# Pooled attention followed by a residual MLP: the first batch issued in single steps from a written list, with the token weights loaded in two transfers

## The chip, the cores and the metric

The kernel runs on one core of a Trainium2 chip. The metric is the device time of one execution in microseconds (us), taken as the median of several runs. A core has five engines that run their own instruction streams and wait for each other through semaphores: TensorE (PE, with its weight loads shown as PEld), VectorE (DVE), ScalarE (ACT), GpSimd (POOL) and SyncE (SP). Transfers between HBM and on-chip memory are issued by SP, ACT and POOL and carried out by 16 transfer engines. A transfer that also changes the type (float32 in HBM, bfloat16 on chip) is issued by GpSimd here.

## The reference, cut to what matters

```python
def attn(q, k, v):                       # each (8 batches, 8 heads, 576, 64), float32
    k_p = k.reshape(B, H, 72, 8, D).mean(axis=3)      # 8 keys pooled into one
    v_p = v.reshape(B, H, 72, 8, D).mean(axis=3)
    scores = (q @ k_p.T) / 8             # 576 x 72 a head
    attn = exp(scores - max) / sum       # softmax
    return attn @ v_p

x = attn(q, k, v) as (8, 576, 512)       # heads side by side
a1 = alpha1 * x + beta1
tok = einsum('ts,bsd->btd', w_tok, a1)   # tokens mixed, w_tok is 576 x 576
u = x + lam * tok
a2 = alpha2 * u + beta2
out = u + lam * (max(a2 @ w_ch1, 0) @ w_ch2)          # 512 -> 2048 -> 512
```

## The kernel before, in words

Tokens are laid out in chunks of 128 rows; a batch has four chunks and a rest of 64 rows, and two batches share one chunk for their rests. Four chunks make a block, and the MLP runs over nine blocks. The main loop (from line 1198) issues block n's MLP and, in between, the attention and token mixing of batch n + 1: each piece of work has a due time written beside it, the pieces are sorted by it, and each is issued whole. Everything before that loop, lines 1054 to 1135, is the first batch: its attention and mixing have no MLP beside them, and their order is the order of the calls. This part is what the change rewrites. Engines run their instructions in the order in which they are issued, so the place of a call sets the place on each engine that it uses.

The pieces of the first batch:

- `att_F` (line 580) transposes a quarter of q on TensorE and copies the result out of PSUM; `att_Frem` does it for the rest rows. `double_k` (629) copies a column of k on VectorE, which the pooling of k needs, and for the first half also converts the rest of k.
- `att_K` (663) pools four heads of k on TensorE (16 small matmuls and 4 for the rest) into one PSUM tile, which two copies move to `kpT`. `first_V` (690) does the same for v.
- `att_S` (712) makes one head's scores: two halves, each a matmul of 256 columns (the second with 64 more for the rest) and one exponential on ScalarE. 16 exponentials make the first batch.
- `att_AV` (773) multiplies with v and normalises on VectorE (`reciprocal`, then `tensor_tensor`) into `x`. `att_X` (801) and `rest_X` (794) multiply x with lam*alpha1, which `spread_lamal` (499) has broadcast to all rows by a float32 matmul and a copy. The results `xs` are the operands of token mixing.
- `setup_wtok` (514) transposes 128 rows of the token weights on TensorE (five transposes) and copies them to `wtT`; `setup_rowsum` (527) adds a row of sums. `setup_vectors` (506) turns beta2 and alpha2 into columns.
- `mix_T` (862) mixes tokens for a chunk: five matmuls of 512 columns, an add on VectorE into `u`, then a scaling with alpha2 into bfloat16 on VectorE or GpSimd. `mix_uT` (881) transposes that chunk for the MLP.
- `mlp_A` (906) makes 128 of the hidden columns; in block 0 it is called for the first 256 tokens (the first half, with a bias column) and the other 256 (the second half, with the activation).

Transfers: all that convert types go through GpSimd's queue, in the order of its calls: the first batch's q, k and v (lines 409 to 447), the token weights (`load_wtok`, 386), the first half of w_ch1 (`load_w1(0)`), the second batch's q and k, the second and third part of w_ch1, the second batch's v (`load_v32`), w_ch2. They use eight completion semaphores in turn, so a transfer also waits until the eighth before it has landed. The second batch's k goes into buffers of the first batch's k and has to wait until that has been pooled; GpSimd's own arithmetic stands behind such an issue in the same queue. Small vectors, the broadcasts of alpha2 and lam and the rests come through SP and ACT (`load_al2`, `load_lam`, `load_rem`; a one-column memset on an engine sets from when they may start).

PSUM has eight banks: six of the pool `psA`, which `gp` (line 240) hands out in turn, and two of `psB`.

Of the kernel before, what the change touches and what calls it, by code (L numbers as in the profile page):

```python
# [7 lines left out]
FP = mybir.dt.float32  # L8
# [6 lines left out]
P = 128  # L15
SPG = 72
# [194 lines left out]
def kernel(  # L211
# [27 lines left out]

    def gp(name):  # L240
        return psA.tile([P, 512], FP, tag="gp", name=name)

# [143 lines left out]
    def load_wtok():  # L386
        nc.gpsimd.dma_start(out=wt_bf[:, 0:4 * S],
                            in_=moe_w_tok[0:512, :].rearrange("(p c) s -> p (c s)", c=4))
        nc.vector.memset(wt_bf[:, 5 * S:], 0.0)
        nc.vector.memset(wt_bf[64:128, 4 * S:5 * S], 0.0)  # L390
        nc.gpsimd.dma_start(out=wt_bf[0:REM, 4 * S:5 * S], in_=moe_w_tok[512:576, :])
# [107 lines left out]
    def spread_lamal(half, copy):  # L499
# [3 lines left out]
        nc.tensor.matmul(out=ps, lhsT=ones_row, rhs=vecs[0:1, 2, cols])  # L503
        copy(out=lamal_bc[:, cols], in_=ps)

    def setup_vectors():
        ps = gp("ps_vec")
        nc.tensor.transpose(out=ps[:, 0:8], in_=b2row, identity=identity[0:8, 0:8])
        nc.scalar.copy(out=b2c_bf, in_=ps[:, 0:4])
        nc.scalar.copy(out=al2_cols, in_=ps[:, 4:8])  # L510
        u_fm[0] = work.tile([P, 4, 2, 258], BF, tag="u_fm", bufs=3, name="u_fm")
        nc.scalar.copy(out=u_fm[0][:, :, 0, 256], in_=ps[:, 0:4])

    def setup_wtok(tcx, copy):
# [5 lines left out]
        for sc in range(5):  # L520
            nc.tensor.transpose(out=ps_w[0:P, trc * sc:trc * sc + trc],
                                in_=strided[:, sc, :] if sc < 4 else w[:, 512:640],
                                identity=identity_bf[0:trc, 0:trc])
        copy(out=wtT[:, 0:5, P * tcx:P * tcx + trc],  # L524
             in_=ps_w[:, 0:5 * trc].rearrange("p (s t) -> p s t", t=trc))

    def setup_rowsum(tcx):
# [4 lines left out]
        for sc in range(5):  # L532
            nc.tensor.matmul(out=ps[:, 0:trc], lhsT=ones_bf if sc < 4 else ones_lo,
                             rhs=wtT[:, sc, cols], start=(sc == 0), stop=(sc == 4))
        nc.scalar.copy(out=wtT[64:65, 4, cols], in_=ps[64:65, 0:trc])
# [44 lines left out]
    def att_F(b, hp, copy=nc.scalar.copy):  # L580
# [4 lines left out]
        if r == 0:  # L585
# [14 lines left out]
        def finish(copy):  # L600
            copy(out=st["qT"][u][:, 4 * r:4 * r + 4, :],
                 in_=ps_q[:, 0:512].rearrange("p (c t) -> p c t", c=4))

        if copy is None:
            return finish
        finish(copy)

    def att_Frem(b, copy=None):
# [14 lines left out]
        for c in range(2):  # L623
            nc.tensor.transpose(out=ps_q[:, 128 * c:128 * c + 128],
                                in_=st["rem"][0][:, c].rearrange("p h d -> p (h d)"),
                                identity=identity_bf)
        copy(out=st["rem_qT"], in_=ps_q[:, 0:256].rearrange("p (c t) -> p c t", c=2))

    def double_k(u):

        nc.vector.tensor_copy(out=st1[0]["k"][u][:, :, 4], in_=st1[0]["k"][u][:, :, 0])
        if u == 0:
            cast_rem_k(nc.vector)
# [29 lines left out]
    def att_K(b, u, copy):  # L663
# [18 lines left out]
        if b:  # L682
            copy(out=kp_pool[u], in_=kp)
            return
        for a in range(2):
            rows = slice(64 * a, 64 * a + 64)
            (copy or (nc.scalar.copy, nc.vector.tensor_copy)[a])(
                out=kpT_pool[u][rows, a], in_=kp[rows])

    def first_V(b, u, copy=nc.vector.tensor_copy):  # L690
# [8 lines left out]
        for c in range(nr):  # L699
            nc.tensor.matmul(out=vp, lhsT=pool_vr if b else pool_vr[0:32],  # L700
                             rhs=rest[:, heads, c], start=False,
                             stop=(c == nr - 1))
        copy(out=vp1_pool[u][:, :, 0:64], in_=vp.rearrange("p (h d) -> p h d", h=4))
# [8 lines left out]
    def att_S(b, h):  # L712
        st = st1[b]
        u, r, hh = h // 4, h // 2 % 2, h % 2
        ET = ET_pool[u][:, h % 4]
        for half in range(2):
            n0, n = 256 * half, 256 + 64 * half
            ps_sc = gp("ps_sc")
            nc.tensor.matmul(out=ps_sc[0:SPG, 0:256], lhsT=kpT_pool[u][:, half, h % 4, :],
                             rhs=st["qT"][u][:, 2 * (h % 4):2 * (h % 4) + 2, :])  # L720
            if half:
                nc.tensor.matmul(out=ps_sc[0:SPG, 256:320], lhsT=kpT_pool[u][:, hh, h % 4, :],
                                 rhs=st["rem_qT"][:, :, h // 2::4].rearrange("p c i -> p i c"))
            nc.scalar.activation(out=ET[:, n0:n0 + n], in_=ps_sc[0:SPG, 0:n],
                                 func=AF.Exp, bias=0.0, scale=0.125)
# [47 lines left out]
    def att_AV(b, h):  # L773
# [13 lines left out]
        nc.tensor.matmul(out=av[:, 4 - 4 * odd, :], lhsT=ET[:, r0:r0 + 128], rhs=vp1[:, h % 4, :])  # L787
        rec = recs[:, h, b, :]
# [53 lines left out]
    u_fm = {}  # L842
# [13 lines left out]
    def keep_warm(count):  # L856
# [461 lines left out]
```

## Time and profile before

| what | value |
|---|---|
| median of 3 runs | 332.59 us (332.14 to 333.85) |
| the profiled execution, its own time | 331.99 us |
| its span in the profile | 330.5 us |
| busy in the span: PE, PEld, DVE, ACT, POOL | 320.9, 206.6, 235.0, 174.5, 117.8 us |
| granted clock of TensorE | 1.00 |
| HBM read, written | 38.57 MB, 9.44 MB |

The span is the profiled execution from its first to its last instruction; the profiled execution's own time is 1.49 us longer than its span and lies 0.60 us under the median. Busy times overlap, as the engines run beside each other. The trace gives start and length of each instruction in us from the span's start, and what ended an engine's idle time before it (`[0.32 <-DMA v<-in_v_dram]`: idle for 0.32 us until that load had landed). Groups of like instructions that follow each other are one row, with their count (`x16`). A tile's name is that of the program without its number, `w` standing for w_ch1 and w_ch2 alike.

### The profile page before, as it was taken

The numbers are of one execution on the slowest core, as the hardware profiler recorded it, in microseconds if no ns is written. First come the engines' busy times: TensorE is split into PE (matmuls) and PEld (weight loads), VectorE is DVE, ScalarE is ACT, GpSimd is POOL, SyncE is SP. The second block draws the span as 40 slices with busy tenths as digits, with TensorE's granted clock in tenths as the row PEclk, the third lists the DMA queues.
The fourth block names the chain that finished last, engine by engine and source line by source line (L and its number), as shares of the span: only waits on it lengthen the run. The fifth ranks groups of instructions, "written<-read, shape, count | busy, mean of one in ns | idle before, by whom it ended". The sixth has DMA issues, their size and how long they took to land.

```text
span 330.5 us, 6433 instructions
## 1 busy us (share of the span) xinstructions
PE 320.9 (97%) x2436; PEld 206.6 (63%) x2467; DVE 235.0 (71%) x495; ACT 174.5 (53%) x323; POOL 117.8 (36%) x142
## 2 busy tenths in 40 slices
PE   8989999999999999999999999999999999999995
PEld 3657764445544567656775676558755866586584
DVE  6764276897769979787869787877788793263263
ACT  1675989459522871288028812682268225703710
POOL 8859625997238001800271026202520560000000
PEclk9999999999999999999999999999999999999999
DMA  7999999957897993399439953998560025003013
GB/s 105 191 219 293 277 180 234 182 134 186 167 258 107 194 178 126 82 242 195 156 80 216 214 161 77 173 202 154 144 170 9 2 51 160 0 2 127 0 34 95
DMA packets 73370, 47.72 MB, mean 144 GB/s; under 512 B 41165, under 2 KB 63829, under 8 KB 73338
## 3 DMA queue, kind: packets, MB, share of 16 engines
q1 hardware_dynamic: 58876, 34.50, 44.8%
q0 software_dynamic: 13856, 12.40, 22.4%
q10 hardware_dynamic: 606, 0.40, 0.5%
q8 instruction: 19, 0.31, 0.4%
q14 instruction: 13, 0.11, 0.1%
HBM read 38.57 MB, written 9.44 MB: 145 GB/s over the span
## 4 chain that ended last, share of the span: by engine, by line
PE 89%; DMA 3%; DVE 3%; POOL 2%; issue 1%; ACT 0%; POOLq 0%
PE ps_h L917 38%; PE ps_w L1033 26%; PE ps_tok L869 11%; PE ps_ch L937 7%; DMA wt_bf<-in_moe_w_tok_dram 3%; PE ps_s L739 2%; PE ps_av L783 2%; DVE w L968 1%; DVE u_sb L873 1%; PE ps_r L746 1%; PE ps_av L787 1%; POOL v L301 0%; POOL k L273 0%; ACT wtT L524 0%; POOL u_bf L879 0%
## 5 line engine op out<-in xcount | busy, mean ns | idle before, releaser
L917 PE MATMUL ps_h<-u_fm,w 128*128 128x512 bf16 (+2 forms) x588 | 131.3, 368 | 1.7 <-DVE u_sb L947 0.6
L924 ACT ACTIVATE H<-ps_h,bias_cols 128x512 bf16<-128x512 f32 x144 | 98.1, 688 | 55.4 <-PE ps_h L917 54.0
L917 PEld LDWEIGHTS <-w 128*128 128x128 bf16 x608 | 65.9, 114 | 51.4 <-issue 3.3
L1033 PEld LDWEIGHTS <-H 128*128 128x128 bf16 x560 | 53.5, 98 | 10.8 <-DVE u_sb L1051 1.2
L877 ACT CAST u_bf<-u_sb 128x512 bf16<-128x512 f32 x32 | 19.8, 618 | 70.7 <-issue 41.8
L1033 PE MATMUL ps_w<-w,H 128*128 128x256 bf16 x448 | 53.6, 273 | 0.0
L805 POOL TENSOR_TENSOR xs<-x_tm,lamal_bc 128x512 bf16<-128x512 f32 x12 | 15.2, 1268 | 105.0 <-DVE x_tm L791 104.5
L1051 DVE TENSOR_TENSOR u_sb<-u_sb,ps_w 128x512 f32<-128x512 f32 x54 | 36.4, 684 | 17.9 <-PE ps_w L1033 17.0
L869 PE MATMUL ps_tok<-xs,wtT 128*128 128x512 bf16 (+2 forms) x193 | 44.5, 380 | 0.7 <-DVE xs L805 0.3
L873 DVE TENSOR_TENSOR u_sb<-x_tm,ps_tok 128x512 f32<-128x512 f32 (+1 forms) x40 | 27.4, 684 | 9.8 <-PE ps_tok L869 9.8
L791 DVE TENSOR_TENSOR x_tm<-ps_av,recs 128x320 f32<-128x320 f32 x64 | 31.5, 491 | 2.7
L768 ACT ACTIVATE ET<-ps_s 72x512 f16<-72x512 f32 x56 | 32.3, 592 | 0.0
L937 PE MATMUL ps_ch<-w,H 128*128 128x512 bf16 x124 | 30.0, 379 | 0.2
L869 PEld LDWEIGHTS <-wtT 128*128 128x128 bf16 (+3 forms) x200 | 17.4, 100 | 16.4 <-issue 1.1
L789 DVE RECIPROCAL recs<-ps_av 128x5 f32<-128x5 f32 x64 | 12.1, 189 | 19.0 <-PE ps_av L787 18.8
L709 DVE TENSOR_TENSOR v_u<-v_u 72x1024 f32<-72x1024 f32 (+1 forms) x24 | 23.6, 985 | 0.2
L1033 PE MATMUL ps_w<-w_t,h_s 128*128 128x256 bf16 x168 | 22.6, 272 | 0.0
L937 PEld LDWEIGHTS <-H 128*128 128x128 bf16 x128 | 11.9, 98 | 13.7 <-issue 0.4
L378 POOL TENSOR_TENSOR k_raw<-k_raw 128x512 f32<-128x512 f32 x14 | 19.1, 1367 | 3.5 <-DMA k_raw<-in_k_dram 3.5
L380 POOL TENSOR_TENSOR k_bf<-k_raw 128x512 bf16<-128x512 f32 x14 | 19.2, 1370 | 1.1
L1002 DVE TENSOR_TENSOR h_s<-H 128x1024 bf16<-128x1024 bf16 x21 | 14.6, 696 | 6.3 <-ACT H L924 5.8
L1033 PEld LDWEIGHTS <-h_s 128*128 128x128 bf16 x168 | 16.4, 98 | 4.1
(165 smaller groups left out, 358.1 us busy)
## 6 DMA issues: line engine op xcount, KB each, us to landing
out_dram<-u_sb SPq DMA_DIRECT2D x29, 256.0 KB, 4.3
k_raw<-in_k_dram SPq DMA_DIRECT2D x12, 512.0 KB, 6.0
v_u<-in_v_dram SPq DMA_DIRECT2D x12, 512.0 KB
q_bf<-in_q_dram POOLq DMA_DIRECT2D x16, 256.0 KB, 6.1
w<-in_moe_w_ch_dram POOLq DMA_DIRECT2D x6, 512.0 KB, 13.3
out_dram<-u_sb SPq DMA_DIRECT2D x11, 128.0 KB, 2.2
w<-in_moe_w_ch_dram POOLq DMA_DIRECT2D x1, 1024.0 KB, 14.5
k_raw<-in_k_dram POOLq DMA_DIRECT2D x2, 512.0 KB, 16.8
```

The costliest lines, as they stand in the source:

```text
L380: eng.tensor_tensor(out=bf, in0=twice[0], in1=twice[1], op=ALU.add)
L709: nc.vector.tensor_tensor(out=out, in0=t[:, :, 0:width], in1=t[:, :, width:2 * width], op=ALU.add)
L768: nc.scalar.activation(out=o, in_=i, func=AF.Exp, bias=0.0, scale=0.125 if b < 3 else 0.125 * 0.125)
L791: nc.vector.tensor_tensor(out=x[:, 1 - odd:6 - odd, dd:dd + D], in0=av[:, :, 0:64], in1=rec.unsqueeze(2).to_broadcast((P, 5, D)), op=ALU.mult)
L869: nc.tensor.matmul(out=ps_tok[p0:p1], lhsT=wtT[0:kk, at, P * c:P * c + p1 - p0], rhs=xs_pool[i][0:kk, sc, :], start=(sc == 0), stop=(sc == 4))
L873: nc.vector.tensor_tensor(out=s["u"][p0:p1, :], in0=x[p0:p1, 1 + c if c < 4 else 5 - 5 * i, :], in1=ps_tok[p0:p1, 0:DM], op=ALU.add)
L877: nc.scalar.copy(out=s["u_bf"], in_=s["u"])
L917: nc.tensor.matmul(out=ps_h[:, t0:t1 + one], lhsT=w1_of(cc, j), rhs=rhs, start=(cc == 0), stop=(cc == 3))
L924: nc.scalar.activation(out=H4[n, j // 4][:, j % 4, :], in_=ps_h, func=AF.Relu, bias=bias_cols[:, j:j + 1], scale=1.0)
L937: nc.tensor.matmul(out=ps, lhsT=H_of(n, j)[:, 128 * m:128 * m + 128], rhs=w2[j // 4][:, j % 4, :], start=(j == 0), stop=(j == NJ - 1))
L1033: nc.tensor.matmul(out=ps, lhsT=stat(j), rhs=moving(j), stop=(j == 7), start=(first and (pp == 0 or alone) and j == 0), skip_group_check=True)
L1051: nc.vector.tensor_tensor(out=o, in0=o, in1=banks[key, "both"], op=ALU.add)
```

## The change

1. The pieces of the first batch become generators that stop (`yield`) between their TensorE part and the copy that empties PSUM, or between add and scaling. `att_S` becomes `scores` for one half of a head. `plan` names every piece, with the engine of its copies, and a written list `order` names the piece that takes its next step. So all parts of the first batch, on all engines, are in a new order. Elsewhere the pieces are run to their end at once (`whole`).
2. Some copies change their engine: the first half's two k copies are both ScalarE's (before one each), the second half's two VectorE's (before ScalarE's), the q rest's copy VectorE's, v's second copy and both lam*alpha copies ScalarE's, of q's four quarters the first three ScalarE's and the last VectorE's (before: first and last ScalarE's). Of the mixing chunks one is scaled by GpSimd (before two). Of the operands, GpSimd makes heads 0 to 3 with their rests (before 0 to 5), VectorE the others.
3. Both lam*alpha broadcasts stand on TensorE ahead of k's pooling (before: between the scores), with two warm matmuls ahead of them. Some of the tiles (`in_pair`) come from the two PSUM banks of `psB`.
4. The token weights come in two transfers, columns 0 to 1216 and 1216 to 2304 of 2304.
5. On GpSimd, `load_k(1, u)` is called from the list, ahead of the operands, as before; the second and third part of w_ch1 follow directly after GpSimd's three operand passes (before: one before and one behind its first scaling). The second batch's v and w_ch2 come after its one scaling.
6. The second batch's bias row is made at the end of the list, and `u_fm[0]` is allocated early.

```diff
+    pair = [False]
     def gp(name):
+        if pair[0]:
+            return psB.tile([P, 512], FP, tag="ch", bufs=2, name=name)
         return psA.tile([P, 512], FP, tag="gp", name=name)
+    def whole(parts):
+        for _ in parts:
+            pass
...
     def load_wtok():
-        nc.gpsimd.dma_start(out=wt_bf[:, 0:4 * S],
-                            in_=moe_w_tok[0:512, :].rearrange("(p c) s -> p (c s)", c=4))
+        main = moe_w_tok[0:512, :].rearrange("(p c) s -> p (c s)", c=4)
+        for c0, c1 in ((0, 2 * S + 64), (2 * S + 64, 4 * S)):
+            nc.gpsimd.dma_start(out=wt_bf[:, c0:c1], in_=main[:, c0:c1])
...
     def setup_wtok(tcx, copy):
...
+        yield
         copy(out=wtT[:, 0:5, P * tcx:P * tcx + trc],
...
-        for a in range(2):
+        for a, copy in enumerate(copies):
+            yield
             rows = slice(64 * a, 64 * a + 64)
-            (copy or (nc.scalar.copy, nc.vector.tensor_copy)[a])(
-                out=kpT_pool[u][rows, a], in_=kp[rows])
+            copy(out=kpT_pool[u][rows, a], in_=kp[rows])
...
-    for u in range(2):
-        load_k(1, u, queue=nc.gpsimd)
-    keep_warm(16)
-    att_F(0, 0)
...
-        mlp_A(0, j, 256, 512)
+    warmed = keep_warm(16)
+    plan = {"dr": once(lambda: cast_rem_k(nc.vector)), "b0": once(lambda: bias_row(0)),
+            "b1": once(lambda: bias_row(1)), "Fr": att_Frem(0, vector),
+            "ve": setup_vectors(), "la": once(lambda: load_al2(nc.vector)),
+            "lr": once(lambda: load_rem(1, behind=nc.vector)),
+            "ll": once(lambda: load_lam(nc.vector)), "lv": once(lambda: load_v32(1)),
+            "wa": once(lambda: keep_warm(2, warmed)), "l1": once(lambda: load_w1(1)), "l2": once(lambda: load_w1(2)),
+            "l3": once(lambda: load_w2(0)), "l4": once(lambda: load_w2(1))}
+    for u in range(2):
+        plan[f"d{u}"] = once(lambda u=u: double_k(u))
+        plan[f"k{u}"] = once(lambda u=u: load_k(1, u, queue=nc.gpsimd))
+    for u, copies in enumerate(((scalar, scalar), (vector, vector))):
+        plan[f"K{u}"] = att_K(0, u, *copies)
+    for u, copy in enumerate((vector, scalar)):
+        plan[f"V{u}"] = first_V(0, u, copy)
+    for u, copy in enumerate((scalar, scalar)):
+        plan[f"s{u}"] = spread_lamal(u, copy)
+    for i, copy in enumerate((scalar, scalar, scalar, vector)):
+        plan[f"F{i}"] = att_F(0, i, copy)
+    for h in range(8):
+        plan[f"S{h}a"], plan[f"S{h}b"] = scores(h, 0), scores(h, 1)
+        plan[f"A{h}"] = att_AV(0, h)
+    for h, n, eng in ((0, 4, nc.gpsimd), (2, 0, nc.gpsimd), (4, 2, nc.vector), (6, 2, nc.vector)):
+        plan[f"X{h}"] = once(lambda h=h, eng=eng: att_X(0, h, h + 2, eng, False))
+        plan[f"R{h}"] = once(lambda h=h, n=n, eng=eng: rest_X(0, h, h + n, eng))
+    for c in range(5):
+        plan[f"W{c}"] = setup_wtok(c, scalar)
+    for c, eng in enumerate((nc.gpsimd, nc.vector, nc.vector, nc.vector)):
+        plan[f"r{c}"] = setup_rowsum(c)
+        plan[f"M{c}"], plan[f"T{c}"] = mix_T(0, c, eng), mix_uT((0, c))
+        plan[f"H{c}"], plan[f"G{c}"] = mlp_A(0, c, 0, 256), mlp_A(0, c, 256, 512)
+    in_pair = "A4 A6 F0 F2 Fr M0 M3 S2b S3b S4a S5b T3 V0 V1 W4 r1 s1".split()
+    order = (
+        "F1 F0 d0 dr wa s1 s0 K0 b0 F1 F0 s1 s0 Fr K0 V0 K0 Fr S3a S1a V0 S0a S2a S3a S0a d1 "
+        "S2b S2a K1 K1 k0 S3b S1a S2b S0b S3b S1b S1b F3 K1 F2 S0b A2 F2 A3 F3 S6a A2 S7a S7a "
+        "A1 S7b V1 k1 la A3 A0 S7b S6a S4a A1 V1 S4b S6b A7 S4a A0 S6b S5a S5b S4b S5b A7 A6 "
+        "W1 W0 S5a A6 A4 A5 W2 W0 W3 A4 lr W4 X2 r0 W1 A5 X6 W3 X4 r1 W2 R6 X0 r3 r0 ve R4 r1 "
+        "r2 W4 R0 l1 l2 M1 M0 r3 ve M1 M1 M3 T1 M0 M3 r2 M3 M2 M0 M2 ll T1 T0 T3 T0 M2 H0 T3 "
+        "H2 T2 H3 H0 H1 T2 H3 lv l3 l4 G3 H1 G1 G3 H2 G2 G0 G1 G2 G0 b1")
+    for name in order.split():
+        pair[0] = name in in_pair
+        next(plan[name], None)
+    pair[0] = False
...
-                todo.append((2.6 + 0.9 * hp, lambda hp=hp: att_F(b, hp)))
+                todo.append((2.6 + 0.9 * hp, lambda hp=hp: whole(att_F(b, hp))))
```

In `order`, a name's first mention issues the piece up to its first `yield` (TensorE's part), the next mention what follows. F, K, V, S, A are the steps of attention, X and R the operands, W and r the token weights, M and T mixing and its transposes, H and G the first and second halves of the first four hidden parts, k, l the loads.

More of the change, by code (lines that the diff above doesn't have):

```diff
@@ L598, in att_F @@
                 identity=identity_bf)
[L600 to L606, printed above, removed]
+        yield
+        copy(out=st["qT"][u][:, 4 * r:4 * r + 4, :],
+             in_=ps_q[:, 0:512].rearrange("p (c t) -> p c t", c=4))
     def att_Frem(b, copy=None):
@@ L661, in pool_k, with att_K @@
             in_=rest_sums[:, :, 2 * u:2 * u + 2])
-    def att_K(b, u, copy):
+    def att_K(b, u, *copies):
         st = st1[b]
@@ L682, in att_K @@
         if b:
[L683 removed]
+            copies[0](out=kp_pool[u], in_=kp)
             return
[L685 removed]
+        for a, copy in enumerate(copies):
+            yield
             rows = slice(64 * a, 64 * a + 64)
[L687 to L688 removed]
+            copy(out=kpT_pool[u][rows, a], in_=kp[rows])
     def first_V(b, u, copy=nc.vector.tensor_copy):
@@ L841 @@
     u_of = {}
-    u_fm = {}
+    u_fm = {0: work.tile([P, 4, 2, 258], BF, tag="u_fm", bufs=3, name="u_fm")}
     def chunk_of(b, c):
@@ L1116, with once @@
[L1116 to L1135 removed]
+    def once(do):
+        do()
+        yield
+    vector, scalar = nc.vector.tensor_copy, nc.scalar.copy
```

143 lines of the change are left out of this document (40 added, 103 removed).

## The prediction

> **What bounds the kernel now.** I read the stretches first, then the chain of work that ended last, then each engine in order of time. Columns of the stretches: start and end, length, then busy time of PE, PEld, DVE, ACT, POOL with their instructions, granted clock, DMA share, GB/s.
>
> ```profile
> 8.00:30.50 22.50, 20.34 (x236) 14.66 (x236) 15.77 (x48) 14.55 (x39) 16.75 (x22) 1.00 1.23 233
> 30.50:62.00 31.50, 31.36 (x275) 19.88 (x277) 17.17 (x47) 27.98 (x51) 18.52 (x20) 1.00 1.04 231
> ```
>
> From 30.5 us on TensorE hardly pauses (0.14 us in 31.5), so the change, which rewrites the work of 8 to 32 us, is worth what it moves the start of the second MLP halves, less what comes too late behind them. The DMA share above 1 up to 62 us says that the transfer engines are full: a transfer issued earlier need not land earlier. The chain (start, length, what) names the limits of the first stretch:
>
> ```profile
> 8.73 10.19 DMA wt_bf<-in_moe_w_tok_dram
> 19.47 1.29 ACT wtT L524 x2
> 22.24 0.39 PE ps_tok L869
> 27.04 1.28 POOL u_bf L879
> 30.54 1.92 PE ps_h L917 x16
> ```
>
> Token weights land at 18.92, ScalarE copies their first two transposes until 20.76, mixing starts at 22.24, and GpSimd's 1.28 us holds the third chunk. The second MLP halves start at **30.54**; that moment I work out anew, all times being us from the span's start.
>
> **The change part by part.** 1. *The head gets later.* First TensorE, then ScalarE:
>
> ```profile
> 7.98 0.61 PE L594 MATMUL ps_q<-identity_bf,q_bf 128*128 128x128 bf16 x8
> 8.42 0.28 PE L624 MATMUL ps_qr<-identity_bf,rem_q 128*128 128x128 bf16 x2
> 10.16 0.60 PE L698 MATMUL ps_v<-v,pool_v 128*72 128x256 f16 x4 [0.32 <-DMA v<-in_v_dram]
> 11.02 0.41 PE L719 MATMUL ps_sc<-qT,kpT 128*72 128x256 bf16 x2
> 12.34 0.69 PE L503 MATMUL ps_bc<-vecs,ones_row 1*128 1x256 f32 x2
> 12.96 0.30 PE L783 MATMUL ps_av<-vp,ET 72*128 72x66 f16 x4
> 13.43 0.63 PE L671 MATMUL ps_kp<-pool_main,k 128*128 128x64 bf16 x16
> 14.00 0.38 PE L594 MATMUL ps_q<-identity_bf,q_bf 128*128 128x128 bf16 x4
> 23.61 1.25 PE L869 MATMUL ps_tok<-xs,wtT 128*128 128x512 bf16 x5
> 24.70 0.39 PE L533 MATMUL ps_rs<-wtT,ones_bf 128*128 128x128 bf16 x4
> ```
>
> ```profile
> 9.88 0.39 ACT L687 CAST kpT<-ps_kp 64x288 bf16<-64x288 f32 x1 [0.89 <-DVE qT L601]
> 11.36 1.89 ACT L724 ACTIVATE ET<-ps_sc 72x256 f16<-72x256 f32 x6 [0.82 <-PE ps_sc L719]
> 16.29 0.58 ACT L601 COPY qT<-ps_q 128x512 bf16<-128x512 bf16 x1
> 17.00 2.02 ACT L724 ACTIVATE ET<-ps_sc 72x256 f16<-72x256 f32 x6
> ```
>
> The eight q transposes still end at 8.42, where the next group starts. Behind them now stand two warm matmuls (five of 512 columns take 24.70 - 23.61 = 1.09, so 0.22 each) and both lam*alpha broadcasts (12.96 - 12.34 = 0.62 each): 8.86, then 10.10. k's pooling takes 14.00 - 13.43 = 0.57: 10.67. Two rest transposes (0.11, two of eight's 0.44), then v's six matmuls, 11.02 - 10.16 = 0.86: 11.64. ScalarE's first k copy is ready before that (0.39 from about 10.85). One score matmul (0.12) and the step to ScalarE (0.22; before, 11.02 to 11.36 for both) put the first exponential at 11.98, **0.62 late**.
>
> 2. *ScalarE's queue closes up.* Before, 16 exponentials ran from 11.36 to 19.02, with four copies between them. Now only one q copy (0.58) and one v copy (0.42, last fence) stand there: 11.98 + 16 x 0.315 (1.89 / 6) + 1.00 = 18.02. Following the waits of the built program step by step I find 0.32 of gaps (k's second half must first be doubled by VectorE, one q copy waits for its transposes): **18.34, 0.68 early**. Loads do not starve it: q's second half had landed by 14.00, where its transposes ran at once, and is wanted at 13.67 (0.33 at most); v's lands at 15.0 (below) and is wanted at 15.18. VectorE takes k's other copies and keeps up: eight normalisations, 0.64 each (18.25 - 17.61, below), from 14.58 to 19.75.
>
> 3. *Token weights in two.* Landings (KB, us from issue) and issues:
>
> ```profile
> v<-in_v_dram POOLq DMA_DIRECT2D x1, 256.0 KB, 7.0
> wt_bf<-in_moe_w_tok_dram POOLq DMA_DIRECT2D x1, 72.0 KB, 9.8
> w<-in_moe_w_ch_dram POOLq DMA_DIRECT2D x1, 512.0 KB, 13.8
> v_main<-in_v_dram POOLq DMA_DIRECT2D x1, 1024.0 KB, 12.2
> ```
>
> ```profile
> 8.00 0.76 POOL L301 DMA_DIRECT2D v<-in_v_dram  x1
> 9.27 0.57 POOL L391 DMA_DIRECT2D wt_bf<-in_moe_w_tok_dram  x1
> 18.02 0.71 POOL L798 TENSOR_TENSOR xs<-x_tm,lamal_bc 64x256 bf16<-64x256 f32 x1
> 20.74 0.79 POOL L560 DMA_DIRECT2D w<-in_moe_w_ch_dram  x1
> 28.27 0.95 POOL L309 DMA_DIRECT2D v_main<-in_v_dram  x1
> 17.24 0.37 SPq L493 DMA_DIRECT2D al_bc<-in_moe_alpha_dram  x1
> ```
>
> v lands at 8.00 + 7.0 = 15.0, all token weights at 18.92. 1216 of 2304 columns, moved evenly, are there at 17.07 (bounds 15.0 and 18.92). Their transposes run behind attention matmuls and end at 18.11, so the copies follow the exponentials: 18.34 + 1.29 = 19.63, where it was 20.76. Even the upper bound would leave the copies at 20.8. The second part keeps 18.92 plus what delays it: alpha2's 256 KB, issued at 17.24 before, is now issued at about 15.3, beside it. Bounds 0 and 0.9 (token weights, 576 KB written from twice as much read, took 3.92 us; 256 KB at the read rate). Nothing shows how much falls beside it; I take the middle, 0.45: 19.4. Transposes, then copies from 20.15 to 21.45; the fourth row sum (5 matmuls, 0.28) ends at 21.80, where mixing starts, 0.44 earlier than 22.24.
>
> The Trainium skill, "DMA: Bandwidth & Descriptors", Rules for kernel authors, advises against cutting a transfer into two over disjoint partition halves, since both use the same engines anyway; Anatomy of one DMA, there, gives each a fixed 2.0 us. Here the 72 KB transfer right behind the large one landed at 19.07, 0.15 after it, which speaks against a further 2 us in a full queue. By that page, as an estimate, the second part would be there at about 20.9 and the second halves at 31.1. For alpha2 the same page (Issuing engines are not separate DMA queues) says that transfers of different issuers interleave on the same 16 engines; at its 436 GB/s it would take 0.6 instead of 0.45, by which the sum would be -0.81.
>
> 4. *Operands.* GpSimd issues second-batch k directly behind q, as before; the extra transfer shifts the ring of eight completion counters by one, so the two k issues now also wait for q's second half and for v (15.0), and GpSimd is free at 15.76. Its three operands (two like the 1.28 above, one 0.71) follow the normalisations and end at 19.2; w_ch1's two issues (0.79 each) come right behind, to 20.8. VectorE's two operands and two rests run from 19.75 to 21.6, under the 21.80.
>
> ```profile
> 17.61 0.20 DVE L789 RECIPROCAL recs<-ps_av 128x5 f32<-128x5 f32 x1 [0.41 <-PE ps_av L787]
> 18.25 0.18 DVE L789 RECIPROCAL recs<-ps_av 128x5 f32<-128x5 f32 x1
> 21.49 0.69 DVE L805 TENSOR_TENSOR xs<-x_tm,lamal_bc 128x512 bf16<-128x512 f32 x1 [0.51 <-ACT wtT L535]
> 33.38 0.16 DVE L920 COPY bias_cols<-ps_h 128x1 f32<-128x1 f32 x1 [2.88 <-PE ps_h L917]
> ```
>
> The 0.51 of idle before VectorE's operand ended as GpSimd's issue of 20.74 ended (21.53). If an issue holds such an operand, the two new ones push it from 19.75 to 20.8, by 1.05; if not, by nothing. The row itself names another releaser, ScalarE, so I charge nothing; 0.2 of it would be covered.
>
> 5. *Mixing and first halves.* Five matmuls take 1.09: chunks are ready at 22.88, 23.97, 25.06 and, after one transpose group (0.22), 26.37. The first chunk's add and scaling on VectorE (0.69 each, the length of the operand above) hold the second's add to 25.2; GpSimd's scaling, 1.28, ends at 26.5, its transposes at 26.8, their copy (0.58) at 27.5. Two first halves (0.44 each), transposes 0.22, two more, and the second halves start at **29.58, 0.96 early**. Only one chunk now goes through GpSimd; the third scaling on VectorE lies under the fourth chunk's matmuls. The bias row moved to the end (one VectorE pass) falls into its 2.88 us pause. The earlier rest loads, the lam load and the tile taken early bind nothing; uncovered, the bias row would cost 0.7.
>
> 6. *What is late next.* w_ch1's and v's transfers stand in the same order in a full queue, so I leave their landings. w_ch1's second part, 20.74 + 13.8 = 34.5, is wanted 36.6 - 0.96 = 35.6 (the bias matmuls of its columns). Second-batch v lands at 28.27 + 12.2 = 40.5.
>
> ```profile
> 40.98 0.68 DVE L325 TENSOR_TENSOR v_main<-v_main 128x512 f32<-128x512 f32 x1
> 43.34 0.43 DVE L326 TENSOR_TENSOR vs<-v_main 128x256 f16<-128x256 f32 x1
> 43.98 0.42 DVE L703 CAST vp<-ps_v 72x256 f16<-72x256 f32 x1 [0.20 <-PE ps_v L700]
> 44.65 0.28 PE L783 MATMUL ps_av<-vp,ET 72*128 72x66 f16 x4
> 36.60 0.66 PE L575 MATMUL ps_bias<-b2c_bf,w 128*128 128x1 bf16 x16
> ```
>
> The sums of v ran from 40.98 to 43.77. They cannot start before 40.5, so they end at 43.3, v's copy at 43.73, and the attention matmuls stand at 43.8 where 0.96 would ask for 43.69. So 44.65 - 43.8 = **0.85** survives, whatever above that the prologue gains.
>
> *Sum:* +0.62 (head) - 1.30 (ScalarE closes up) = -0.68; -0.28 more from there to the second halves (first weights earlier, second part delayed, one GpSimd scaling fewer); +0.11 (v). -0.85: 331.99 becomes 331.14 for the profiled execution. The median of the runs, 332.59, is 0.60 above it, so **331.7**.
>
> **The rivals.** A, *v is no gate* and the second weight part is not delayed: second halves at 29.13, gain 1.41, up to 1.7: 331.1. For: v's issue moves from 28.27 to 26.5. Against: the full queue. B, *VectorE's operands are held by the two issues* (the 0.51 row): 1.05 less 0.2, mixing at about 22.6, gain 0.1 to 0.4: 332.3. C, *the second weight part is late*: ScalarE has nothing to copy after 19.63, so each us of landing beyond 19.0 moves all that follows by one, and from 20.4 on the kernel is slower than before. Full alpha2 (0.9), one more issue (0.57) and the rest's 0.15 put it at 20.5 and the second halves at 30.7: 0.15 slower, 332.8. Against: the 0.15. D, *the list does nothing for ScalarE*: the old 7.66 us behind the later head end at 19.64, second weight copies at 22.2, gain 0.2: 332.4.
>
> **How the numbers follow.** Forecast (gain 0.4 to 1.3) 0.50, A 0.18, B 0.14, C 0.10, D 0.08. Half a per cent, about what a measurement of this kernel can tell from no change, is 1.66 us. A's upper part, with runs that differ (332.14 to 333.85 before), gives 0.18 for faster; C beyond its price, and a loss behind 62 us that I don't see, 0.11 for slower; 0.71 within. The range reaches from a gain of 2.2 (there w_ch1's 34.5 would stop TensorE) to C with one 0.51 of B's row on top: 330.4 to 333.2.
>
> **What would show it.** Right: first exponential near 12.0, last one ended near 18.3, the first weight copy there; mixing from 21.4 to 21.8; second halves near 29.6; VectorE waiting for v until 40.5. Wrong: second halves after 30.5; weight copies waiting beyond 20.2 for their transposes (C); VectorE idle up to the end of GpSimd's issues (B); attention matmuls at 43.3 or before (A); pauses of TensorE behind 45 us that were not there.

## The result, and the profile after

The changed kernel takes **329.91 us** (median of 14 runs, 329.51 to 331.57), the kernel before, run beside it, 331.25 us (14 runs, 330.72 to 333.85): a ratio of 0.9952, 95% interval 0.9935 to 0.9969, so 0.3 to 0.7% faster. By the medians 1.34 us are gained, by the ratio about 1.6. The prediction was 331.7 us, a gain of 0.85, and its range ended at 330.4. Of the 1.79 us by which the time is lower than predicted, 1.34 are the level from which it counted: the median of the three runs, 332.59, was that much above the median of the 14 (that this equals the gain is chance). The other 0.45 us is gain that was not foreseen. Ratios count fast runs only: beside some experiments a few runs of the kernel before take 335.6 to 338.7 us at a lower granted clock.

The profiled execution of the changed kernel is the longest of its 14 (331.57 us, span 330.1). Its stretches and its rows of the first 30 us, in order of time and across engines:

```profile
8.00:30.50 22.50, 21.30 (x242) 15.15 (x243) 16.33 (x50) 15.45 (x40) 15.20 (x21) 1.00 1.23 232
30.50:62.00 31.50, 31.50 (x277) 19.72 (x275) 18.41 (x49) 27.98 (x51) 18.41 (x19) 1.00 1.05 231
```

```profile
12.61 1.52 ACT L733 ACTIVATE ET<-ps_sc 72x256 f16<-72x256 f32 x5 [0.63 <-PE ps_sc L727]
...
14.97 0.62 PE L606 MATMUL ps_q<-identity_bf,q_bf 128*128 128x128 bf16 x8 [0.34 <-DMA q_bf<-in_q_dram]
...
17.82 1.73 ACT L733 ACTIVATE ET<-ps_sc 72x256 f16<-72x256 f32 x5
19.58 2.48 ACT L535 COPY wtT<-ps_w 128x640 bf16<-128x640 bf16 x4
...
22.38 3.41 PE L880 MATMUL ps_tok<-xs,wtT 128*128 128x512 bf16 x15
...
29.26 2.81 PE L931 MATMUL ps_h<-u_fm,w 128*128 128x257 bf16 x24
```

TensorE works 0.96 us more in the first stretch (21.30 instead of 20.34) and no longer pauses in the second. The group of 29.26 is eight matmuls of first halves and sixteen of second halves, so the second halves start 0.88 us into it (two groups of four, 0.44 each), at 30.14: only 0.40 us earlier than the 30.54 of before. But q's second half came late here: its transposes waited until 14.97 us and ran at 14.00 before. One execution of each kernel is too little for a difference of 1 us. So I ran the changed kernel again.

### The profile page after: what moved, and what is told of

The parts are those of the page before. It is cut to its first block, busy times and chain, and to the rows that moved or that the text cites. A ratio compares the mean times of both kernels' runs of the same rounds, so it can differ in the third digit from the quotient of the medians.

```text
span 330.1 us, 6467 instructions
## 1 busy us (share of the span) xinstructions
PE 323.3 (98%) x2469; PEld 206.7 (63%) x2469; DVE 235.9 (71%) x497; ACT 175.6 (53%) x324; POOL 115.5 (35%) x140
## 4 chain that ended last, share of the span: by engine, by line
PE 81%; DVE 7%; DMA 5%; POOL 3%; issue 1%; ACT 1%; SPq 0%; POOLq 0%; DVEq 0%
PE ps_h L931 34%; PE ps_w L1048 23%; PE ps_tok L880 10%; PE ps_ch L952 7%; DMA kT<-k_bf 2%; DMA q_bf<-in_q_dram 2%; PE ps_av L792 2%; PE ps_s L748 2%; DVE w L983 1%; DVE u_sb L885 1%; DVE x_tm L801 1%; DVE H L1017 1%; POOL k_bf L388 1%; DVE u_sb L1066 1%; POOL k_raw L386 1%
## 5 line engine op out<-in xcount | busy, mean ns | idle before, releaser
L931 PE MATMUL ps_h<-u_fm,w 128*128 128x512 bf16 (+2 forms) x608 | 132.7, 368 | 0.5 <-DVE u_sb L962 0.2
L815 POOL TENSOR_TENSOR xs<-x_tm,lamal_bc 128x512 bf16<-128x512 f32 x11 | 13.9, 1270 | 104.8 <-DVE x_tm L801 104.7
L880 PE MATMUL ps_tok<-xs,wtT 128*128 128x512 bf16 (+3 forms) x200 | 44.5, 380 | 0.0
L386 POOL TENSOR_TENSOR k_raw<-k_raw 128x512 f32<-128x512 f32 x14 | 18.7, 1334 | 3.2 <-DMA k_raw<-in_k_dram 3.1
L388 POOL TENSOR_TENSOR k_bf<-k_raw 128x512 bf16<-128x512 f32 x14 | 19.1, 1364 | 1.1
```

Source lines behind the costliest of these rows:

```text
L386: eng.tensor_tensor(out=raw[:, :, 0:2], in0=raw[:, :, 0:2], in1=raw[:, :, 2:4], op=ALU.add)
L388: eng.tensor_tensor(out=bf, in0=twice[0], in1=twice[1], op=ALU.add)
L880: nc.tensor.matmul(out=ps_tok[p0:p1], lhsT=wtT[0:kk, at, P * c:P * c + p1 - p0], rhs=xs_pool[i][0:kk, sc, :], start=(sc == 0), stop=(sc == 4))
L931: nc.tensor.matmul(out=ps_h[:, t0:t1 + one], lhsT=w1_of(cc, j), rhs=rhs, start=(cc == 0), stop=(cc == 3))
```

## The experiments

All times are medians; beside each stands the ratio to runs of the kernel before on the same chip, with its 95% interval.

### The changed kernel again: c_again, c_again2

Edit: none.

> The changed kernel once more, to see an ordinary execution of it (the profiled one of the result was the longest of 14, with q's second half landing only near 14.9 us). Theory of the prediction (v's landing lets only 0.85 us through): second MLP halves near 29.6 us, second-batch v lands near 40.5, VectorE waits for it, attention matmuls of the second batch near 43.8, about 0.85 us under the kernel before. Rival (neither the second weight part nor v is a gate): second halves at 29.1 or earlier, attention matmuls at 43.3 or earlier, 1.4 to 1.6 us under the kernel before.

> The changed kernel once more, for a third trace of it. If the second halves start when ScalarE's last exponential ends plus constants: mixing 2.84 us behind it, second halves 7.75 us behind that, end 300.7 to 301.5 us behind those, whatever the landings of this execution are.

Measured: c_again 330.18 us, ratio 0.9959 (0.9938 to 0.9981); its profiled execution took 329.56 us. c_again2 gave one time, 329.86 us. Rows of c_again in order of time, across engines:

```profile
11.14 1.52 ACT L733 ACTIVATE ET<-ps_sc 72x256 f16<-72x256 f32 x5 [0.53 <-PE ps_sc L727]
13.12 1.14 ACT L733 ACTIVATE ET<-ps_sc 72x320 f16<-72x320 f32 x3 [0.46 <-PE ps_sc L730]
...
16.30 1.73 ACT L733 ACTIVATE ET<-ps_sc 72x256 f16<-72x256 f32 x5
18.06 2.48 ACT L535 COPY wtT<-ps_w 128x640 bf16<-128x640 bf16 x4
18.25 1.00 PE L531 MATMUL ps_w<-identity_bf,wt_bf 128*128 128x128 bf16 x15
20.87 3.41 PE L880 MATMUL ps_tok<-xs,wtT 128*128 128x512 bf16 x15
...
27.74 2.81 PE L931 MATMUL ps_h<-u_fm,w 128*128 128x257 bf16 x24
...
38.70 0.46 DVE L690 CAST kp<-ps_kp 128x288 bf16<-128x288 f32 x1 [3.51 <-PE ps_kp L684]
39.57 0.69 DVE L333 TENSOR_TENSOR v_main<-v_main 128x512 f32<-128x512 f32 x1 [0.42 <-DMA v_main<-in_v_dram]
...
42.30 0.42 DVE L711 CAST vp<-ps_v 72x256 f16<-72x256 f32 x1
42.77 0.29 PE L792 MATMUL ps_av<-vp,ET 72*128 72x66 f16 x4
```

Read it from the top. ScalarE's last exponential ends at 18.03 and the first weight copy follows at 18.06. The transposes of the second weight part run at 18.25 with no wait, and four copies stand back to back (2.48 us). Mixing starts at 20.87 and the second halves at 27.74 + 0.88 = 28.62. VectorE then does wait for v, 0.42 us, but v is there at 39.57, not at 40.5, and the attention matmuls start 14.15 us behind the second halves, against 44.65 - 30.54 = 14.11 before. c_again2 confirms the constants: first weight copy 18.64, mixing 21.44, second halves 29.20.

### The kernel before again: b_again, b_again2

Edit: none.

> The kernel before once more, for a second trace of it. If its prologue is set by the landing of all token weights: first weight copy 0.4 to 0.7 us behind the last exponential again, mixing 3.2 us behind it, second halves 8.3 us behind that, second halves between 30.0 and 30.8 us.

> The kernel before once more, since the last trace of it had a granted clock of 0.50 from 11 to 24 us. With the clock at 1.00: last exponential ended near 19, first weight copy 0.4 to 0.7 us behind it, mixing 3.2 us behind it, second halves 8.3 us behind that, between 30.0 and 30.8 us.

Measured: 335.07 and 332.89 us, one time each. b_again fell into something that none of the theories held (stretches of three microseconds; the columns are those of the prediction, the granted clock third from the end):

```profile
7.00:10.00 3.00, 1.77 (x30) 1.29 (x31) 1.95 (x10) 1.05 (x3) 3.00 (x6) 1.00 1.46 196
10.00:13.00 3.00, 2.93 (x21) 2.36 (x21) 2.05 (x6) 1.93 (x7) 2.54 (x4) 0.73 1.44 193
13.00:16.00 3.00, 3.00 (x37) 2.29 (x37) 1.46 (x4) 1.23 (x4) 0.51 (x2) 0.50 1.18 217
```

TensorE was busy for only 1.77 of 3 us while it waited for q, k and v. Its clock was 0.50 from about 11.4 to 25 us; mixing started at 26.14 and the second halves at 34.44. b_again2 kept its clock:

```profile
19.42 1.29 ACT L524 COPY wtT<-ps_w 128x640 bf16<-128x640 bf16 x2
...
22.00 1.25 PE L869 MATMUL ps_tok<-xs,wtT 128*128 128x512 bf16 x4
...
30.30 0.93 PE L917 MATMUL ps_h<-u_fm,w 128*128 128x256 bf16 x7 [0.23 <-DVE bias_cols L920]
```

Second halves at 30.30, as expected. But the weights were not late: no idle time stands before the copy, and mixing follows it 2.58 us later. In the kernel before, weights and exponentials finish almost together, and which is last changes from run to run: the one transfer landed near 18.9 us in the profile of before and near 17.8 in b_again2 (10.2 and 9.1 us from issue).

### The token weights in one or two transfers: c_one, b_two

```diff
-        for c0, c1 in ((0, 2 * S + 64), (2 * S + 64, 4 * S)):
+        for c0, c1 in ((0, 4 * S),):
```

(c_one; b_two makes the opposite edit in the kernel before.)

> The changed kernel with the token weights in one transfer again. Theory of the prediction (ScalarE runs out of exponentials at 18.3 us and wants weights then): all weights land at 18.9 to 19.4, the five copies run from about 19.3 to 22.2 instead of 18.3 to 21.5, 0.7 us later than the changed kernel. Rival (ScalarE is still busy with exponentials when all weights are there, as in the profiled execution, whose last exponential ended at 19.55): no more than 0.1 us either way.

> The kernel before with the split of the token weights alone. If the split carries the gain: the first weight copy moves from 19.47 to 19.02 us, where the last exponential ends, and at most 0.45 us are gained. If the second part is late: its copies wait beyond 20.3 and nothing or less than nothing is gained. If the written list carries the gain: within 0.3 us of the kernel before.

Measured: c_one 331.30 us, ratio 0.9982 (0.9966 to 0.9997); b_two 332.03 us, ratio 1.0005 (0.9986 to 1.0024). c_one, run beside c_again, is 1.12 us slower by the medians and 0.8 by the means of 12 runs, with ratio intervals that overlap:

```profile
18.31 0.75 PE L531 MATMUL ps_w<-identity_bf,wt_bf 128*128 128x128 bf16 x10 [0.67 <-DMA wt_bf<-in_moe_w_tok_dram]
...
19.10 1.29 ACT L535 COPY wtT<-ps_w 128x640 bf16<-128x640 bf16 x2 [0.89 <-PE ps_w L531]
...
21.91 0.38 PE L880 MATMUL ps_tok<-xs,wtT 128*128 128x512 bf16 x1
```

With one transfer ScalarE, done with its exponentials at 18.21, stands for 0.89 us. This is the wait that the split takes away; the 0.7 expected for it is of the right size. In the order of before the split is worth nothing that these runs can tell, although the trace of b_two shows the first copy without idle time, at 18.84: ScalarE reaches the weights later there (18.84 against 18.55 in the mean, below), and in b_again2 they were there in one transfer too.

### The head: c_kfirst, c_nowa

```diff
-        "F1 F0 d0 dr wa s1 s0 K0 b0 F1 F0 s1 s0 Fr K0 V0 K0 Fr S3a ..."
+        "F1 F0 d0 dr wa K0 s1 s0 b0 F1 F0 K0 s1 s0 Fr V0 K0 Fr S3a ..."
```

(c_kfirst; c_nowa drops only `wa`.)

> The changed kernel with k's pooling ahead of the two lam*alpha broadcasts on TensorE, and its first copy ahead of theirs on ScalarE. If the later head (0.62 us by the prediction) is on the path: first exponential 0.4 to 0.7 us earlier and the same amount gained in all. If loads (q's second half, v) or the landing of second-batch v set the end: first exponential earlier, but less than 0.2 us gained.

> The changed kernel without the two warm matmuls ahead of the lam*alpha broadcasts. By the price of the prediction (0.22 us of TensorE in the head): first exponential 0.2 us earlier, at most 0.2 us gained. Rival (they bridge a pause in which TensorE's clock would fall, as in c_kfirst, where TensorE paused 0.6 us for k and the granted clock was 0.90, 0.50 and 0.88 from 10 to 18 us): granted clock under 0.95 somewhere between 8 and 16 us and 0.3 to 0.7 us lost. Third case (loads set the first exponential): within 0.1 us.

Measured: c_kfirst 330.78 us, ratio 0.9970 (0.9950 to 0.9991); c_nowa 330.58 us, ratio 0.9978 (0.9960 to 0.9997). Neither gains; both medians are 0.4 to 0.6 us above c_again's, with intervals that overlap its own. In c_kfirst TensorE waited 0.60 us for k:

```profile
7.00:10.00 3.00, 2.20 (x31) 1.54 (x32) 1.89 (x9) 1.19 (x3) 3.00 (x6) 1.00 1.44 197
10.00:13.00 3.00, 3.00 (x17) 1.92 (x17) 1.42 (x4) 1.90 (x6) 2.64 (x4) 0.76 1.43 191
13.00:16.00 3.00, 3.00 (x48) 2.77 (x47) 1.49 (x5) 2.33 (x8) 1.46 (x3) 0.67 1.20 213
```

Its first exponential came at 12.47, not earlier than in the changed kernel. What the prediction counted as 0.62 us of delay is also cover: the two broadcasts fill time in which k is still under way. The clock fell in four of the 12 runs (granted clock of the whole run 0.993 or 0.994, 331.0 to 331.9 us); the median of the other eight, 330.2, is that of c_again. So without the loss of clock the order of the head is worth nothing that these runs can tell. c_nowa's trace shows a clock of 1.00 up to 24 us, and only two of its 12 runs have one under 0.997; whether it loses anything, and by what, stays open.

### k's second half later, v earlier: c_k1late, c_vearly, c_both

```diff
-  ... S2b S2a K1 K1 k0 S3b S1a S2b S0b S3b S1b S1b F3 ...   # c_k1late
+  ... S2b S2a S3b S1a S2b S0b S3b S1b S1b K1 K1 k0 F3 ...
-  ... R0 l1 l2 M1 ... H3 lv l3 l4 ...                       # c_vearly
+  ... R0 l1 lv l2 M1 ... H3 l3 l4 ...
```

> The changed kernel with the pooling of k's second half on TensorE behind the first half's remaining scores. In c_again TensorE stood 0.35 us for k's second half (landed 11.95) with three scores behind it, and ScalarE idled 0.46 us. If ScalarE's queue sets when the weight copies and so mixing start: that idle goes, and 0.3 to 0.5 us are gained. If the weights' landing (second part near 18.1 us) or v's landing sets the end: first weight copy earlier, but less than 0.15 us gained.

> The changed kernel with second-batch v issued ahead of w_ch1's third part and ahead of GpSimd's scaling. Theory of the prediction (v's landing is the gate behind a gain of about 0.85 us): with 512 KB less ahead of it v lands about 2.2 us earlier (512 KB at the 232 GB/s of that stretch), VectorE no longer waits for it, and up to 0.4 us are gained, the wait that c_again shows. Rival (v is no gate: in all six traces so far the attention matmuls of the second batch start 14.11 to 14.15 us behind the second MLP halves): v lands as early, the 14.1 stays, gain below 0.1 us; a loss if w_ch1's third part comes too late.

> c_vearly and c_k1late together. If v's landing hides what c_k1late gains, this one gains it: 0.4 to 0.8 us under the changed kernel. If v is no gate, it equals c_k1late within 0.15 us.

Measured: c_k1late 330.40 us, ratio 0.9943 (0.9913 to 0.9974); c_vearly 331.49 us, 1.0004 (0.9983 to 1.0025); c_both 331.14 us, 0.9993 (0.9978 to 1.0007). c_k1late cannot be told from the changed kernel: its exponentials run without the 0.46 us pause, but the next three wait 0.31 us, since their q lands late. c_vearly loses the whole gain, and not by v. On GpSimd:

```profile
25.39 0.76 POOL L572 DMA_DIRECT2D w<-in_moe_w_ch_dram  x1 [4.08 <-DMA w<-in_moe_w_ch_dram]
26.17 1.27 POOL L892 TENSOR_TENSOR u_bf<-u_sb,al_bc 128x512 bf16<-128x512 f32 x1
```

v is two transfers; with both ahead, the issue of w_ch1's third part is the one that has to wait until w_ch1's first part has landed (eight completion counters in turn), and GpSimd's scaling stands behind it in the queue. TensorE waited 1.9 us for that scaling, and its clock then fell to 0.50; in c_both it waited 0.9 and kept its clock. So the times of this pair don't tell what an earlier v is worth, but the traces do: v landed near 37.4 us in both (issue near 20, 17.6 and 17.3 us to landing), and the attention matmuls still start 14.12 us behind the second halves (45.86 - 31.74, 43.93 - 29.81). With v early that distance stays at the 14.11 of before.

### What a late v costs: c_v2

```diff
-  ... H3 lv l3 l4 G3 ...
+  ... H3 l3 lv l4 G3 ...
```

> The changed kernel with one of the w_ch2 transfers (512 KB) issued ahead of second-batch v. v lands about 2.2 us later, near 42.0 us. Theory of the prediction (from a landing on v needs 3.3 us to the attention matmuls, and PE waits there): attention matmuls near 45.2, 16.5 instead of 14.1 us behind the second MLP halves, and 1.5 to 2.2 us lost. Rival (TensorE or later stages give that wait back): attention matmuls late, but less than 0.7 us lost in all.

Measured: 333.20 us, ratio 1.0057 (1.0035 to 1.0078).

```profile
42.33 0.69 DVE L333 TENSOR_TENSOR v_main<-v_main 128x512 f32<-128x512 f32 x1 [2.72 <-DMA v_main<-in_v_dram]
...
45.52 0.29 PE L792 MATMUL ps_av<-vp,ET 72*128 72x66 f16 x4 [0.26 <-DVE vp L711]
```

Second halves at 29.07, attention matmuls at 45.52: 16.45 us behind them, 2.3 more than the 14.15, and 3.19 behind v's landing. The gate is real and its distance (3.3 us in the prediction) right; the changed kernel stands just at its edge, since v lands at 39.5 to 40.5 us there. The loss, 3.0 us against c_again, is more than the 1.5 to 2.2 expected. Eight of the 12 runs had a granted clock of 0.990 to 0.995; the other four have a median of 332.7, 2.5 above c_again, which is near the wait.

### GpSimd's scalings: c_gp2, c_gpm2, b_gp1, b_twogp1

```diff
-    for c, eng in enumerate((nc.gpsimd, nc.vector, nc.vector, nc.vector)):
+    for c, eng in enumerate((nc.gpsimd, nc.vector, nc.vector, nc.gpsimd)):   # c_gp2
+    for c, eng in enumerate((nc.gpsimd, nc.vector, nc.gpsimd, nc.vector)):   # c_gpm2
-    mix_T(0, 2, nc.gpsimd)
+    mix_T(0, 2)                                     # b_gp1; b_twogp1 with b_two's edit too
```

> The changed kernel with two of the four scalings on GpSimd, as before (here the first chunk of the list and the third). By the prediction's step 5 (one GpSimd scaling fewer is worth 0.52 us between the start of mixing and the second halves, 8.30 us before, 7.75 in c_again): 8.1 to 8.4 us from mixing to the second halves, 0.4 to 0.6 us lost. Rival (VectorE, which it relieves of 1.03 us, sets that stretch): 7.75 or less, nothing lost.

> The changed kernel with the last chunk of the list scaled on GpSimd too, behind the one that is there already (c_gp2 put the two in a row, the later one first, so it did not price one scaling). By step 5: GpSimd's 1.27 us instead of VectorE's 0.69 hold the last transposes, 8.1 to 8.4 us from mixing to the second halves, 0.4 to 0.6 us lost, and no fall of the clock, since TensorE pauses less than 1 us.

> The kernel before with its third chunk scaled on VectorE, so that GpSimd has one scaling, as in the changed kernel. By the prediction's step 5 (one GpSimd scaling fewer: 8.30 us from mixing to the second halves become 7.78): about 0.5 us gained. Rival (the list's order of the chunks is what does it): less than 0.2 us.

> The kernel before with one GpSimd scaling and with the token weights in two transfers, but without the written list. If the gain is that of the weights' landing and of the scaling, and the list's order on ScalarE adds nothing (rival D of the prediction): as fast as the changed kernel, 1.2 to 1.6 us under the kernel before. If the list is needed: 0.3 to 0.9 us under it.

Measured: c_gp2 333.21 us, ratio 1.0048 (1.0024 to 1.0072); c_gpm2 330.66 us, 0.9987 (0.9971 to 1.0004); b_gp1 331.54 us, 1.0008 (0.9982 to 1.0035); b_twogp1 331.37 us, 0.9987 (0.9967 to 1.0007). c_gpm2 is the clean test: TensorE waits for GpSimd's scaling,

```profile
PE ps_uT L906 <- POOL u_bf L892: 0.4, 1, 0.4
```

and from mixing (20.98) to the second halves (28.42 + 0.88 = 29.30) it takes 8.32 us instead of 7.75: 0.57, with 0.52 predicted. In c_gp2 the two scalings stood in a row with the later chunk's first, so it doesn't price one scaling; TensorE waited 2.0 us and lost its clock as well:

```profile
25.00:28.00 3.00, 0.96 (x10) 0.52 (x9) 2.47 (x3) 0.17 (x1) 3.00 (x3) 1.00 1.25 320
28.00:31.00 3.00, 2.55 (x18) 2.07 (x17) 0.16 (x1) 1.49 (x3) 3.00 (x7) 0.66 1.10 307
```

In the order of before, one scaling fewer gives only 0.12 (mixing 21.39, second halves 29.57, 8.18 instead of 8.30): there two row sums, 0.28 us each, stand on TensorE between the chunks. Split and scaling together without the list do not reach the changed kernel by the ratio, though the intervals (from 0.9967 here, to 0.9969 there) just touch. That rival D, the list does nothing for ScalarE, falls is plainer from its rows: from the start of the first exponential to the end of the last it takes 6.6 to 6.9 us in the changed kernel, 7.7 before.

### TensorE's wait near 68 us: c_klate, b_kearly

```diff
-                    at = (15.31 if b == 1 else 21.0) + 0.01 * u
+                    at = (16.6 if b == 1 else 21.0) + 0.01 * u     # c_klate; b_kearly: 14.6
```

> The changed kernel with the third batch's k issued by SyncE behind that batch's v instead of ahead of it, so that it lands some 2 us later. In the traces so far TensorE's wait near 68 us (for VectorE's last passes over u) follows the moment at which GpSimd starts on that k, counted from the second MLP halves: up to 27.2 us behind them 0 to 0.2 us, 27.2 to 27.5 us 0.2 to 0.6, beyond 27.6 us 0.8 to 0.9. If that contention between GpSimd's and VectorE's passes is the part of the gain that the prediction missed: wait of 0.6 us or more near 68 us, 0.5 us or more lost in all. If the wait hangs on the prologue alone: 0 to 0.2 us, nothing lost.

> The kernel before with the third batch's k issued about 2 us earlier (ahead of that batch's rests). Both traces of it so far wait 0.6 us near 68 us. If GpSimd's start on that k sets the wait: start 26.7 us or less behind the second halves, wait 0 to 0.2 us, 0.4 to 0.6 us gained without any change of the first batch. If not: 0.6 us, nothing gained.

Measured: c_klate 337.62 us (6 runs), ratio 1.0183 (1.0142 to 1.0223); b_kearly 331.16 us, 0.9990 (0.9966 to 1.0013). c_klate went wrong for another reason. The late k holds GpSimd's cast of the rests, SyncE's transposition of the rests waits for that cast, and the transposition of u that the next block needs stands behind it in SyncE's queue:

```profile
PE ps_h L931 <- DMA u_fm<-u_bf: 5.2, 1, 5.2
```

In b_kearly the wait of 0.6 us near 68 us is gone from the trace, as expected, but the gain of 0.3 us lies within its interval. So it is not shown that this wait has a part in the result.

## Why the prediction was wrong

The prologue of the changed kernel is in five traces (its own, c_again, c_again2, c_v2, c_klate, which differ only behind it), that of the kernel before in three with a full clock (its own, b_again2, b_kearly):

| us | first weight copy | mixing | second halves |
|---|---|---|---|
| before: profile, b_again2, b_kearly | 19.47, 19.42, 19.31 | 22.24, 22.00, 22.08 | 30.54, 30.30, 30.38 |
| changed: profile, c_again, c_again2, c_v2, c_klate | 19.58, 18.06, 18.64, 18.50, 17.96 | 22.38, 20.87, 21.44, 21.31, 20.77 | 30.14, 28.62, 29.20, 29.07, 28.53 |
| difference of the means | -0.85 | -0.75 | **-1.30** |
| predicted, against the profile of before | -1.13 | -0.44 | -0.96 |

1. **The head and ScalarE's queue (steps 1 and 2): right in kind.** First exponential forecast at 11.98: 11.14 to 12.61 in the five traces, 11.81 in the mean. First weight copy forecast at 18.34: 18.55 in the mean. That these agree so well is partly luck: the queue from the one to the other was forecast to take 6.36 us and takes 6.59 to 6.97, 6.74 in the mean, but starts 0.17 earlier. The list closes ScalarE's queue, with more gaps than were worked out; five traces of the same instructions spread over 1.6 us, the latest being that in which q's second half landed late.
2. **The second weight part (step 3): this is the step that failed.** It was to land at 19.4, 0.45 of that by alpha2 beside it, and to stop the copies until 20.15. In none of the five traces does a copy or transpose of it wait. From the first copy to mixing were forecast 3.46 us and are 2.81, the same in all five within 0.01. It landed near 19.1, 18.1, 17.2, 18.4 and 18.0 us (issue near 9.3; the order is that of the table), 18.2 in the mean. Two things were mis-sized. The 18.92 that the step starts from is one execution's: the single transfer landed near 18.9, 17.8, 18.7 and 17.2 us in the profile of before, b_again2, b_kearly and b_gp1 (before's kernel up to mixing), and near 18.2 in c_one, 18.2 in the mean too. And alpha2, issued at 14.9 to 16.6 us in the five and at 17.2 to 17.8 before, shows no delay: its 0.45 was the middle of two bounds, 0 and 0.9; the runs are near 0. The margin can be thin: in c_again the part landed near 18.1 and its transposes ran at 18.25. The second part in c_again, then the single transfer in b_gp1 (KB, us from issue):

```profile
wt_bf<-in_moe_w_tok_dram POOLq DMA_DIRECT2D x1, 272.0 KB, 8.8
```

```profile
wt_bf<-in_moe_w_tok_dram POOLq DMA_DIRECT2D x1, 576.0 KB, 8.5
```

3. **The operands (step 4): right.** VectorE's two operands run while GpSimd issues, without a pause, here in c_again; rival B falls.

```profile
19.11 1.54 POOL L572 DMA_DIRECT2D w<-in_moe_w_ch_dram  x2
19.49 1.28 DVE L815 TENSOR_TENSOR xs<-x_tm,lamal_bc 128x512 bf16<-128x512 f32 x2
```

4. **From mixing to the second halves (step 5): right.** 7.78 forecast, 7.75 or 7.76 measured, and c_gpm2 puts the scaling at 0.57.
5. **v (step 6): the mechanism right, the landing wrong.** From 40.5 on, v would have taken back 0.11 and capped the gain at 0.85. It landed at 39.57 in c_again (issue 25.47), near 39.5 in c_again2, near 39.7 in c_klate, at 40.5 only in the profiled execution. The queue is full, but v issued 1.3 to 2.9 us earlier still comes up to 0.9 earlier. It cost 0.04 in c_again (14.15 - 14.11), 0.01 and 0.02 in the profile and c_again2, and 0.28 in c_klate, whose second halves start earliest of the five, at 28.53 (VectorE, then TensorE):

```profile
39.73 0.69 DVE L333 TENSOR_TENSOR v_main<-v_main 128x512 f32<-128x512 f32 x1 [0.69 <-DMA v_main<-in_v_dram]
...
42.92 0.29 PE L792 MATMUL ps_av<-vp,ET 72*128 72x66 f16 x4
```

6. **The level.** The sum's last term, the median 0.60 above the profiled execution, came from three runs. By the 14 the median of before, 331.25, lies 0.74 below the profiled 331.99. This is the larger part of the miss of the time, and it says nothing of the change.

The sum by the runs: -0.85 (ScalarE) + 0.10 (copies to mixing, 2.71 becomes 2.81; 0.69 was forecast) - 0.54 (to the second halves) + 0.09 (v, the mean of the four) = -1.20, beside a measured gain of 1.34 by the medians and 1.0 to 2.2 by the ratio's interval. The -0.85 rests on means of traces that differ by up to 1.6 us among themselves, so it is known to some tenths at best; with b_gp1, c_gp2 and c_gpm2 added, which run the same instructions up to mixing, it is -0.86 (first weight copies 18.81, 17.82 and 18.18). This is nearest to rival A, second halves at 29.13 and a gain of 1.41, which had 0.18; but v is still a gate at times, as c_klate shows. Rival C (a late second part) falls with step 3. What remains between 1.20 and the ratio's 1.6 isn't settled. TensorE's wait near 68 us is 0.6 us in the profile of before and in b_again2, 0 to 0.2 in c_again, c_again2 and the changed kernel's profile, and was no part of the sum; but b_kearly, which removes it, shows no certain gain.

The Trainium skill, "DMA: Bandwidth & Descriptors", Rules for kernel authors, speaks of halves over disjoint partitions; this cut is by columns, and the traces are against carrying the rule over: in c_one, without it, ScalarE waits 0.89 us, not because the bytes come later (all had landed near 18.2 us, the second part of c_again near 18.1) but because none can be used before that; the first part of c_again had landed near 16.0. The estimate of 20.9 us for the second part, from the same page, fails with the transposes of 18.25.

## What to carry to other kernels

Splitting a load pays where its consumer has run out of other work before the whole load is there: here the split took away a wait of 0.9 us behind the new order and was worth nothing that the runs can tell behind the old one. Take the level of a prediction from many runs, and a difference below 1% from several traces of each kernel: the second halves of one and the same prologue lie 1.6 us apart in five traces, and one and the same transfer landed 1.7 us apart. Before a transfer is issued earlier, count which transfer must have landed before its successor may be issued, and what arithmetic stands behind that on the issuing engine.

## What the runs showed of the hardware that was not expected

**TensorE's clock can fall after a stretch without a long pause, and does not always.** Busy for 1.77 of 3 us (b_again, longest pause 0.60 us) it had a granted clock of 0.50 from about 11.4 to 25 us; for 2.20 of 3 us (c_kfirst, 0.60 us) 0.76 and 0.67 in the next two stretches. But b_twogp1 was busy for only 1.32 of the same 3 us, with a pause of 1.17, and kept 1.00:

```profile
7.00:10.00 3.00, 1.32 (x18) 0.85 (x16) 1.16 (x8) 0.59 (x1) 3.00 (x6) 1.00 1.43 198
10.00:13.00 3.00, 3.00 (x38) 2.32 (x39) 2.35 (x8) 2.02 (x7) 2.64 (x4) 1.00 1.43 191
```

So neither the busy share of such a stretch nor its longest pause decides it, and what does stays open. Pauses of 1.9 and 2.0 us (c_vearly, c_gp2) were followed by 0.50 from about 27.4 to 30.8 and from 29 to 32.4 us, one of 0.9 (c_both) by 1.00. So a pause of TensorE can cost more than its length, and work in front of a late load need not be mere delay. The Trainium skill, "TensorE: Matmul & The Clock Gate", Part 1, has the half clock follow an idle window of about 3.4 us; the 0.50 agrees, but here no stretch of that length was idle.

**VectorE beside GpSimd.** Two of VectorE's passes over w_ch2 take 1.28 us while GpSimd is idle (c_klate) and 2.36 beside its arithmetic (before). Transfers don't explain it: they moved 384 GB/s during the fast pair and 162 during the slow one.

```profile
60.87 1.28 DVE L983 TENSOR_TENSOR w<-w,lam_bc 128x512 bf16<-128x512 bf16 x2
```

```profile
62.59 2.36 DVE L968 TENSOR_TENSOR w<-w,lam_bc 128x512 bf16<-128x512 bf16 x2
```

So a load for GpSimd that lands a little earlier or later changes the speed of an engine that doesn't use it.
